# VectorE and ScalarE in the order as written for the first quarter of tokens, key-value products one unit later

## The chip, the cores and the metric

One core of a Trainium2 chip runs the whole program. The time is the device time of one execution in microseconds (us).

## The reference, cut to what matters

Four layers: linear attention, gated MLP, linear attention, gated MLP, each with a layer norm ahead and a residual sum behind, on 2048 tokens of width 1024. Only the first attention layer matters here:

```python
qkv = layernorm(x) @ wqkv                 # 32 heads of 32
phi = lambda t: where(t > 0, t + 1, exp(t)) + 1e-6
kv  = einsum("bhsd,bhse->bhde", phi(k), v)   # summed over all tokens
z   = einsum("bhsd->bhd", phi(k))            # summed over all tokens
o   = (phi(q) @ kv) / (phi(q) @ z + 1e-6)
x   = x + o @ wo
```

## The kernel before

Tokens are handled in tiles of 128; four tiles are a quarter. A "unit" is eight TensorE matmuls that project one tile onto 512 columns. Every unit is followed by a tick, and `later.at(n, f)` runs `f` n ticks on. In the first quarter of layer 0 there are eight value units, then eight key units; after the second key unit of a tile comes its key-value step, eight small matmuls that add phi(k)ᵀ v of that tile.

```python
def phi(self, ps, out):                       # after each key unit
    nc.scalar.activation(out=e, in_=ps, func=ACT.Exp)                    # L243
    nc.vector.tensor_scalar(out=e, in0=e, ..., op0=ALU.min, op1=ALU.add) # L244, first half
    nc.vector.scalar_tensor_tensor(out=out, in0=ps, ..., in1=e, ...)     # L245, second half
...
def k_sum(t):                                 # column sums for z, on GpSimd
    nc.gpsimd.tensor_tensor(out=ksum, in0=ksum, in1=pk[t], op=ALU.add)   # L299 (first one L297)
...
def v_unit(q, j, c):                          # ScalarE copies a value unit out of PSUM
    nc.scalar.activation(out=va[t][...], in_=project(f"v{c}", q, j), func=ACT.Copy)  # L304
...
def last(j):                                  # second key unit of a tile
    u_j = u[QT + j]
    return lambda: (u_j(), later.at(3, lambda: kv_step(q * QT + j)))
...
for i in range(QT, self.ST):                  # layer norms of tiles 4 to 15, three ticks apart
    self.ln_at((4 if l == 0 else 2) + 3 * (i - QT), l, i, 2)
...
run(first)                                    # eight value units
run(k_then_kv(0))                             # eight key units
run(column_major(v_unit, 1))
run(k_then_kv(1))
```

A layer norm is two statistics instructions and an aggregation on VectorE (L136, L141), two small ones on ScalarE for the reciprocal deviation (`rstd`, L143, L144), and a scaling on VectorE (L152). Where nothing says otherwise, a scheduler decides at build time in which order each engine gets its instructions, by its own estimate of when each could run. A region with `manual_schedule(engines=...)` makes those engines take the instructions of the region in the order in which the program issues them; what stands outside the region is still placed by the scheduler. TensorE writes its products to a memory called PSUM; the PSUM tiles for units come from a pool of four. "The head" is the start of the kernel, up to the transposes of the first four token tiles. In the profile lines `x` is the input, `xn` a normalized tile, `tp` and `xnT` its transposes, `ps` a unit's result, `e` the exponential in phi, `pkv` a buffer of phi(k) and v, `kv` the key-value products and `ksum` the column sums.

Of the kernel before, what the change touches and what calls it, by code (L numbers as in the profile page):

```python
# [15 lines left out]
QT = 4  # L16
# [62 lines left out]
class _Net:  # L79
# [184 lines left out]
    def layer_A(self, l, last_ln):  # L264
        nc, G, KT, D = self.nc, self.G, self.KT, self.D
        ring, later = self.ring, self.later
# [40 lines left out]
        def kv_step(t):  # L307

            for g in range(G):
                b, i = divmod(g, NW // P)  # L310
                nc.tensor.matmul(kv[b][:, i * P:(i + 1) * P], lhsT=pk[t][:, g * P:(g + 1) * P],  # L311
                                 rhs=va[t][:, g * P:(g + 1) * P], start=(t == 0 and i == 0),
                                 stop=(t == self.ST - 1 and i == NW // P - 1),
                                 skip_group_check=True)
# [86 lines left out]
        def column_major(f, q):  # L401
            return [lambda j=j, c=c: f(q, j, c) for c in range(H) for j in range(QT)]
# [16 lines left out]
        def k_then_kv(q):  # L419
            u = column_major(k_unit, q)  # L420

            def last(j):
                u_j = u[QT + j]
                return lambda: (u_j(), later.at(3, lambda: kv_step(q * QT + j)))

            return u[:QT] + [last(j) for j in range(QT)]

        def run(*lists):

            n = max(len(u) for u in lists)  # L430
            for i in range(n):
                for u in lists:
                    if i < len(u):
                        u[i]()
                        later.tick()
# [7 lines left out]
        first = column_major(v_unit, 0)  # L443
        if l == 0:

            first = [first[c * QT + j] for c, j in ((0, 0), (0, 1), (1, 0), (0, 2), (1, 1), (1, 2),
                                                    (0, 3), (1, 3))]
        run(first)
        run(k_then_kv(0))
        run(column_major(v_unit, 1))  # L450
        run(k_then_kv(1))
        run(column_major(k_unit, 2))
# [154 lines left out]
```

## Time and profile before

| | before |
|---|---|
| device time, median of 6 runs | 1644.81 us (1644.57 to 1646.01) |
| profiled span | 1642.6 us |
| TensorE busy | 1632.7 us |
| TensorE's wait for phi of the first quarter | 0.6 us |
| TensorE's wait at the transposes of token tile 3 | 1.5 us |

How to read it: TensorE has work in all but 9.9 us of the span, so the table of its waits, not the busy shares of the others, says what there is to win. A line of that table names who waited, the line and releaser, and then total, number and longest of the waits. The prediction shows these lines. The wait in the head: this is the timeline of the kernel before around it (start, duration, engine, line, operation, and in brackets the idle time before and who ended it):

```profile
16.45 0.69 DVE L136 BATCH_NORM_STATS2 stats<-x 128x6 f32<-128x512 bf16 x1 [1.33 <-DMA x<-in_A_x_dram]
17.07 0.19 DVE L141 BATCH_NORM_AGGREGATE mv<-st 128x2 f32<-128x12 f32 x1
...
18.46 0.62 PE L203 MATMUL tp<-ident,xn 128*128 128x128 bf16 x8 [1.53 <-DVE xn L152]
```

VectorE stands still for 1.33 us for the input of tile 4 (written to `stats`), and only then aggregates tile 3 (read from `st`), whose statistics were long there. TensorE then waits for tile 3.

### The profile page before, as it was taken

The page shows a single profiled execution, that of the slowest core. Times are in us where ns is not written, and L with a number is a line of the kernel's source. Part 1 is how long each engine was busy: PE and PEld are TensorE (multiplying, and loading weights), DVE is VectorE, ACT ScalarE, POOL GpSimd, SP SyncE. Part 2 cuts the span into 40 slices and gives each one's busy share as a digit, 9 for nine tenths or more (in the row PEclk, how much of TensorE's full clock was granted, in tenths as well). Part 3 has the DMA queues.
Part 4 walks back from the last instruction along what each step waited for, and adds up shares of the span by engine and source line. Part 5 has one row for each costly group of instructions (what it writes and reads, how often), then busy time and mean ns, then how long its engine had stood idle before and what let it go on. Part 6 is the DMA issues. An engine that isn't in the chain of part 4 may idle for free.

```text
span 1642.6 us, 18754 instructions
## 1 busy us (share of the span) xinstructions
PE 1632.7 (99%) x7786; PEld 749.8 (46%) x7786; DVE 575.8 (35%) x931; ACT 371.7 (23%) x699; POOL 196.3 (12%) x102
## 2 busy tenths in 40 slices
PE   8999999999999999999999999999999999999999
PEld 4444444444444444444444444444444444444444
DVE  8654876222211311322146457841112112211111
ACT  4356602101110110111033675121011101101110
POOL 0355800000000000000013566000000000000000
PEclk9999999999999999999999999999999999999999
DMA  9113726456445544644530146374544564455452
GB/s 283 25 52 78 181 42 171 149 166 195 152 138 167 160 151 157 183 151 142 166 77 1 58 104 154 55 202 145 176 143 153 160 198 150 144 158 163 154 160 71
DMA packets 298052, 227.18 MB, mean 138 GB/s; under 512 B 103152, under 2 KB 296048, under 8 KB 297968
## 3 DMA queue, kind: packets, MB, share of 16 engines
q1 hardware_dynamic: 293216, 221.80, 46.7%
q10 hardware_dynamic: 4752, 4.20, 0.8%
q8 instruction: 61, 1.00, 0.3%
q14 instruction: 23, 0.19, 0.0%
HBM read 197.13 MB, written 4.19 MB: 123 GB/s over the span
## 4 chain that ended last, share of the span: by engine, by line
PE 94%; ACT 2%; DVE 1%; issue 1%; ACTq 0%
PE pg L508 24%; PE pu L508 24%; PE acc L532 23%; PE ps L284 16%; PE ps L390 7%; PE kv L311 1%; ACT e L347 1%; ACT e L346 1%; PE acc_last L532 0%; DVE den L361 0%; DVE pq L349 0%; ACT e L348 0%; PE fold L378 0%; DVE T L384 0%; DVE xn L152 0%
## 5 line engine op out<-in xcount | busy, mean ns | idle before, releaser
L508 PEld LDWEIGHTS <-t 128*128 128x128 bf16 x3584 | 350.7, 98 | 422.8
L508 PE MATMUL pg<-xnT,t 128*128 128x512 bf16 x1792 | 423.3, 379 | 0.0
L508 PE MATMUL pu<-xnT,t 128*128 128x512 bf16 x1792 | 423.3, 379 | 0.0
L532 PE MATMUL acc<-t,hT 128*128 128x512 bf16 x1764 | 382.5, 379 | 0.0
L514 DVE TENSOR_TENSOR hT<-pu,rg 128x512 bf16<-128x512 f32 x224 | 154.7, 691 | 571.6 <-PE pu L508 571.6
L284 PE MATMUL ps<-t,xnT 128*128 128x512 bf16 x1536 | 341.0, 379 | 1.0 <-DVE xnT L206 0.6
L513 ACT ACTIVATE rg<-pg 128x512 f32<-128x512 f32 x224 | 133.6, 596 | 737.5 <-PE pg L508 737.4
L532 PEld LDWEIGHTS <-hT 128*128 128x128 bf16 x1820 | 178.1, 98 | 209.0
L284 PEld LDWEIGHTS <-xnT 128*128 128x128 bf16 x1536 | 148.7, 98 | 175.2 <-issue 1.8
L390 PE MATMUL ps<-T,pqT 128*128 128x512 bf16 x512 | 111.2, 379 | 0.0
L143 ACT ACTIVATE rstd<-mv,eps 128x1 f32<-128x1 f32 x64 | 18.9, 295 | 339.9 <-DVE mv L141 339.9
L297 POOL CAST ksum<-pkv 128x1024 f32<-128x1024 bf16 x2 | 2.3, 1136 | 682.8 <-DVE pkv L245 682.8
L547 DVE TENSOR_TENSOR xo<-x,acc 128x512 bf16<-128x512 f32 x31 | 21.3, 687 | 170.3 <-PE acc L532 170.3
L136 DVE BATCH_NORM_STATS2 stats<-x 128x6 f32<-128x512 f32 (+1 forms) x120 | 78.4, 671 | 2.0 <-DMA x<-in_A_x_dram 1.3
L390 PEld LDWEIGHTS <-pqT 128*128 128x128 bf16 x512 | 50.1, 98 | 60.4
L356 POOL TENSOR_TENSOR prod<-pq,zrow 128x1024 f32<-128x1024 bf16 x32 | 68.1, 2127 | 58.2 <-DVE den L361 35.9
L544 DVE TENSOR_TENSOR x<-x,acc 128x512 f32<-128x512 f32 x32 | 21.6, 676 | 149.5 <-PE acc L532 148.4
L299 POOL TENSOR_TENSOR ksum<-ksum,pkv 128x1024 f32<-128x1024 f32 x30 | 65.5, 2182 | 68.9 <-DVE pkv L245 67.7
L244 DVE TENSOR_SCALAR e<-e 128x512 f32<-128x512 f32 x64 | 52.8, 825 | 48.8 <-ACT e L243 48.5
L349 DVE SCALAR_TENSOR_TENSOR pq<-ps,e 128x512 bf16<-128x512 f32 x64 | 42.9, 670 | 68.3 <-ACT e L348 68.2
L367 POOL TENSOR_TENSOR pq<-pq,den 128x1024 bf16<-128x1024 bf16 x32 | 61.2, 1912 | 10.5 <-issue 4.0
L243 ACT ACTIVATE e<-ps 128x512 f32<-128x512 f32 x64 | 38.1, 596 | 70.8 <-PE ps L284 68.0
(46 smaller groups left out, 490.4 us busy)
## 6 DMA issues: line engine op xcount, KB each, us to landing
t<-in_B_W_gate_dram SPq DMA_DIRECT2D x56, 1024.0 KB, 6.6
t<-in_B_W_up_dram SPq DMA_DIRECT2D x56, 1024.0 KB, 5.3
t<-in_B_W_down_dram SPq DMA_DIRECT2D x64, 896.0 KB, 5.1
t<-in_A_wqkv_dram SPq DMA_DIRECT2D x11, 1024.0 KB, 5.1
t<-in_A_wo_dram SPq DMA_DIRECT2D x4, 1024.0 KB, 5.2
out_dram<-xo ACTq DMA_DIRECT2D x31, 128.0 KB, 2.2
x<-in_A_x_dram SPq DMA_DIRECT2D x15, 256.0 KB, 8.2
t<-in_A_wqkv_dram SPq DMA_DIRECT2D x2, 512.0 KB, 4.9
```

Of the source, the lines that this page charges most:

```text
L136: self.nc.vector.bn_stats(out=stats[:, c, :], in_=src[:, c * fmax:(c + 1) * fmax])
L244: nc.vector.tensor_scalar(out=e, in0=e, scalar1=1.0, scalar2=1e-6, op0=ALU.min, op1=ALU.add)
L284: nc.tensor.matmul(ps, lhsT=self.xnT[l, l_q][:, kt, j * P:(j + 1) * P], rhs=w[:, kt, :], start=(kt == 0), stop=(kt == KT - 1))
L299: nc.gpsimd.tensor_tensor(out=ksum, in0=ksum, in1=pk[t], op=ALU.add)
L349: nc.vector.scalar_tensor_tensor(out=pq[:, c * NW:(c + 1) * NW], in0=ps, scalar=0.0, in1=e, op0=ALU.max, op1=ALU.add)
L356: nc.gpsimd.tensor_tensor(out=prod, in0=pq, in1=zrow, op=ALU.mult)
L367: nc.gpsimd.tensor_tensor(out=heads(pq), in0=heads(pq), in1=den[:, :].unsqueeze(2).to_broadcast([P, D // HD, HD]), op=ALU.mult)
L390: nc.tensor.matmul(ps, lhsT=pqT[sc][:, g, j * P:(j + 1) * P], rhs=T[g // 2][:, g % 2, n2 * NW:(n2 + 1) * NW], start=(g == 0), stop=(g == G ...
L508: nc.tensor.matmul(ps, lhsT=w[:, kt, fi * P:(fi + 1) * P], rhs=self.xnT[l, q][:, kt, :], start=(kt == 0), stop=(kt == KT - 1))
L513: nc.scalar.activation(out=rg, in_=pg, func=ACT.Relu)
L514: nc.vector.tensor_tensor(out=h[:, fi, :], in0=pu, in1=rg, op=ALU.mult)
L532: nc.tensor.matmul(ps[:, 0:n], lhsT=hT[ft // 4][:, ft % 4, j * P:(j + 1) * P], rhs=wd[:, k, i * n:(i + 1) * n], start=(ft == 0), stop=(ft ...
```

## The change

The intent: keep the layer norms of later tiles from standing in front of phi in VectorE's queue, and give phi one unit more before TensorE uses it.

```diff
             def last(j):
                 u_j = u[QT + j]
-                return lambda: (u_j(), later.at(3, lambda: kv_step(q * QT + j)))
+                return lambda: (u_j(), later.at(4, lambda: kv_step(q * QT + j)))
 ...
-        run(first)
-        run(k_then_kv(0))
+        def quarter0():
+            run(first)
+            run(k_then_kv(0))
+
+        if l == 0:
+            with self.tc.manual_schedule(engines={mybir.EngineType.DVE,mybir.EngineType.Activation}):
+                quarter0()
+        else:
+            quarter0()
         run(column_major(v_unit, 1))
```

## The prediction

> **What bounds the kernel now.** I read the page's busy shares first, then the waits of TensorE over the whole span, then busy time by stretch for the first 70 us, then the timeline around the one wait that the change can reach. The page's first lines:
>
> ```profile
> span 1642.6 us, 18754 instructions
> ## 1 busy us (share of the span) xinstructions
> PE 1632.7 (99%) x7786; PEld 749.8 (46%) x7786; DVE 575.8 (35%) x931; ACT 371.7 (23%) x699; POOL 196.3 (12%) x102
> ```
>
> TensorE is busy 1632.7 of 1642.6 us: 9.9 us idle in all, and the matmuls are the same after the change. So no reordering of other engines can gain more than 0.6% of the time. TensorE's waits, whole span:
>
> ```profile
> PE idle L174 <- DVE zero L171: 2.1, 1, 2.1
> PE tp L203 <- DVE xn L152: 1.5, 1, 1.5
> PE fold L378 <- DVE T L384: 1.5, 4, 0.4
> PE kv L311 <- DVE pkv L245: 0.6, 1, 0.6
> ```
>
> (Columns: total, times, longest.) The first two lie in the head (start and transposes of the first four token tiles), the third after the query projections. Only the fourth, one wait of 0.6 us of a key-value product for phi(k), is of the stage that the change touches. Busy time by stretch (window: length, then busy time of each engine):
>
> ```profile
> 18.00:27.00 9.00, 8.54 (x46) 4.19 (x47) 8.96 (x22) 5.10 (x16) 0.00 (x0) 1.00 1.07 371
> 27.00:36.00 9.00, 9.00 (x44) 4.03 (x43) 8.96 (x21) 4.08 (x12) 0.00 (x0) 1.00 1.20 216
> 36.00:48.00 12.00, 11.40 (x77) 6.06 (x76) 11.55 (x22) 4.54 (x13) 8.17 (x4) 1.00 0.64 110
> 48.00:58.00 10.00, 10.00 (x48) 4.56 (x47) 0.55 (x1) 4.13 (x8) 0.00 (x0) 1.00 0.28 53
> ```
>
> From 18 to 48 us VectorE (third busy figure) is full: it runs the layer norms of tiles 5 to 15 far ahead of their use, woven between the phi of the first eight key units; then it is idle for 9.4 us. TensorE loses 0.60 us in 36:48, nothing in 27:36 and 48:58. How the loss arises (timeline):
>
> ```profile
> 39.15 4.89 POOL L299 TENSOR_TENSOR ksum<-ksum,pkv 128x1024 f32<-128x1024 f32 x2 [0.45 <-DVE pkv L245]
> ...
> 41.56 0.50 DVE L244 TENSOR_SCALAR e<-e 128x512 f32<-128x512 f32 x1
> ...
> 41.98 2.35 DVE L152 TENSOR_SCALAR xn<-x,mv,rstd 128x1024 bf16<-128x1024 bf16 x1
> ...
> 44.24 0.68 DVE L245 SCALAR_TENSOR_TENSOR pkv<-ps,e 128x512 bf16<-128x512 f32 x1
> ...
> 44.98 0.40 PE L311 MATMUL kv<-pkv 128*128 128x128 bf16 x4 [0.60 <-DVE pkv L245]
> ```
>
> A layer-norm scaling (L152), not needed for many microseconds, stands between the two halves of the last phi. It takes 2.35 us instead of the 0.55 us it takes elsewhere, because GpSimd's column sum (L299) is running; the phi ends at 44.92 and the product starts 0.60 us late.
>
> **What the Trainium skill says.** "SBUF — State Buffer", section Who interferes with whom: VectorE's 2-port modes, open to tensor_scalar, take a port pair shared with GpSimd as an exclusive lock, and the later one fully blocks; VectorE work with at most one SBUF input outside those modes is not affected. The trace agrees: L152 above ends just after GpSimd's pair of sums (39.15 + 4.89 = 44.04), while the second half of phi (L245, one input in PSUM) stays at 0.68 us beside GpSimd. "PSUM — Partial Sum Buffer", section Engine vs sequencer instructions: ScalarE and VectorE queues are strict FIFO. Agreed, and it carries this case: the L245 that TensorE awaited stood behind L152.
>
> **The change, part by part.** I compared the instruction orders before and after. TensorE: the same products, each tile's eight key-value matmuls one unit of eight matmuls later. GpSimd and SyncE: unchanged orders. VectorE and ScalarE: different only up to the last layer norm of layer 0; the second attention layer shifts only its key-value products, where no wait was seen. Nothing is added or removed, so the sum is a change of TensorE idle time before about 65 us.
>
> Durations I use, from timeline rows: a unit of TensorE 1.725 us (ScalarE exps 57.50, 59.23, 60.95), a kv step 0.44 (37.48 to 37.92), exp 0.60, first half of phi 0.42, second half 0.69 (together about 1.07 in a row), a layer norm on VectorE 1.71 per tile (scalings at 23.48, 25.20, 26.91), GpSimd's sum 2.15.
>
> (a) First key units. VectorE now does only tiles 4 and 5 early, then waits for the exp of key unit 0. Unit n of k ends at 27.3 + 1.725n. Phi 0 ends about 29.1, phi 1 30.9; then tile 6's norm in between (stats 30.8 to 32.1, rstd, scaling 33.4), phi 2 to 4 by 36.7, tile 7's norm to 39.3, then phi 5 40.4, phi 6 41.4. GpSimd starts the sum of tile 1 at 40.7, so the first half of phi 7 (ready at 41.4) is held to 43.2 as above, and phi 7 ends about 43.9.
>
> (b) Products. With the extra unit kv0 to kv3 stand at 39.4, 41.5, 43.7, 45.9, after phi 4 to 7 at 36.7, 40.4, 41.4, 43.9: slack 2.7, 1.1, 2.3, 2.0. No wait: **-0.60 us**. Without the extra unit kv1 would stand near 39.8, before its phi at 40.4: some 0.6 us lost. So the reordering alone would gain nothing; the extra unit is what pays.
>
> (c) The norms pushed back. Tiles 8 to 15, eight times 1.71 to 1.77 us = 14 us, now start at 43.9 instead of running from 20 us on, and end near 59.7 instead of 48.7. Their outputs have time: tile 8 is first used by unit 24 of TensorE, near 70 us. But ScalarE's order interleaves their rstd pairs with the copies of the next eight value units, and a copy frees one of four PSUM tiles for the unit four later. Adding up: copies of value units 1, 2, 3 start near 46.3, 48.4, 52.2 and must end by 49.8, 51.5, 53.2 (slack 3, 2.5, 0.4 us); the copies of units 4 to 6 wait for the stats of tiles 12, 13, 14 and end near 55.0, 56.8, 58.6, against key units that want to start at 54.9, 56.7, 58.4. That is a tie: VectorE's 1.71 us per tile against TensorE's 1.725 per unit. My sum gives **+0.2 us** new idle; one microsecond of later VectorE would make it about +1.1, one earlier 0. Tile 8's scaling also meets GpSimd's last sum (45.4 to 47.5) and is blocked about 0.7 us, which is in the sum.
>
> (d) Phi of the next key units waits for the norms' end: first one near 61.3, needed at 62.1. No loss.
>
> Sum: -0.60 + 0.2 = **-0.4 us**: 1644.9 us.
>
> **The rivals.** (1) ScalarE's copies held behind the pushed-back statistics become TensorE's new wait (step c), +1 to +2 us: for it, the tie; against it, the same weave ran at 24 to 27 us without any wait of TensorE. It would make 1645.5 to 1646.5. (2) GpSimd's lock hits a first half of phi worse than I reckon, so kv3 waits: 2.0 us slack is nearly a whole sum, so less likely; 1645 to 1646. (3) The wait goes away with nothing new: 1644.7. (4) The head's 1.5 us wait (a tile-4 statistics op put ahead of tile 3's aggregation) might be thought cured; the order of those instructions is the same in both, so it stays. (5) The transposes into the next quarter come late: tile 7's is scaled at 39.3, lands 3.3 us later (median of DMA landings of xnT), 42.6, and is needed at 46.3: no.
>
> **Range and chances.** The three runs before spread 1.4 us (1644.61 to 1646.01), as much as the effects. From rival 3 with half the spread below, to rival 1 with some above: 1643.6 to 1646.6. Two per cent is 33 us, more than three times all idle time of TensorE, so faster is impossible by this and slower would need a stall that no step has.
>
> **What would show it.** Right: no wait of kv (L311) for L245 in TensorE's waits; GpSimd's first column sum near 36.9 instead of 37.46; VectorE idle from about 26 to 28 us and full from 44 to 60; the 1.5 us wait of tp unchanged. Wrong: TensorE waits of L284 for ScalarE's pkv copies (L304) between 50 and 60 us larger than 0.5 us in sum, or a kv wait still there. The prediction as a whole fails if TensorE's idle time changes by more than about 1.5 us either way.

## The result, and the profile after

The changed kernel took 1644.03 us (median of 6, 1643.65 to 1644.63), the kernel before 1644.81 us. The ratio, 0.9994 with a 95% interval of 0.9982 to 1.0007, is the mean time of the one kernel's fast runs over that of the other's of the same rounds, so not quite the ratio of these medians. The interval holds 1: the clocked time alone does not prove a gain. A second set of five runs gave 1643.86 us against 1645.07 us (ratio 0.9993, 0.9979 to 1.0007). The traces are sharper than the clock. TensorE's waits in the changed kernel, whole span:

```profile
PE idle L174 <- DVE zero L171: 2.1, 1, 2.1
PE tp L203 <- DVE xn L152: 1.7, 2, 1.3
PE fold L378 <- DVE T L384: 1.5, 4, 0.4
PE ps L284 <- DVE xnT L206: 0.3, 1, 0.3
```

The wait of L311 for L245 is gone and no wait for L304 has come. (Of the two waits of `tp`, 1.30 us is at tile 3 and 0.38 us at tile 1.) Busy time by stretch (window: length, then TensorE, weight loads, VectorE, ScalarE and GpSimd, then granted clock, busy share of the DMA engines and GB/s):

```profile
18.00:27.00 9.00, 8.22 (x44) 4.03 (x46) 3.57 (x9) 4.44 (x11) 0.00 (x0) 1.00 1.07 371
27.00:36.00 9.00, 8.96 (x42) 4.07 (x42) 6.44 (x13) 3.26 (x7) 0.00 (x0) 1.00 0.77 150
36.00:48.00 12.00, 11.93 (x79) 6.44 (x80) 11.19 (x20) 3.75 (x10) 7.52 (x4) 1.00 0.14 26
48.00:58.00 10.00, 9.95 (x47) 4.55 (x47) 9.84 (x23) 4.61 (x16) 0.00 (x0) 1.00 0.70 132
```

VectorE's work has moved: 3.57 us instead of 8.96 in 18:27, and 9.84 instead of 0.55 in 48:58. TensorE's busy figure must not be compared across the two traces: this one has 7632 matmul records where the other has 7786, for the same program, so some are missing. I use start times instead. Timeline of the changed kernel around the products:

```profile
39.47 0.61 PE L311 MATMUL kv<-pkv 128*128 128x128 bf16 x8
...
40.71 6.64 POOL L299 TENSOR_TENSOR ksum<-ksum,pkv 128x1024 f32<-128x1024 f32 x3 [2.73 <-DVE pkv L245]
...
41.53 1.63 DVE L244 TENSOR_SCALAR e<-e 128x512 f32<-128x512 f32 x1
...
43.19 0.69 DVE L245 SCALAR_TENSOR_TENSOR pkv<-ps,e 128x512 bf16<-128x512 f32 x1
...
45.99 0.61 PE L311 MATMUL kv<-pkv 128*128 128x128 bf16 x8
```

GpSimd still delays VectorE here (1.63 us for the first half of the last phi, where the same step took 0.42 us just before it). But that phi ends at 43.88 us, 2.1 us before its product at 45.99.

**The stage as a ruler.** From the start of the tile-3 transposes (`tp`) to the first key-value product of the second quarter TensorE does the same work in both kernels, apart from the one extra unit (8 matmuls at 0.2158 us, 1.73 us) that now comes first. The lines before (the `tp` at 18.46 is shown further up; the line at 44.00 is the first half of the product that waits) and after:

```profile
44.00 0.39 PE L311 MATMUL kv<-pkv 128*128 128x128 bf16 x4
...
67.66 0.61 PE L311 MATMUL kv<-pkv 128*128 128x128 bf16 x8
```

```profile
18.72 0.62 PE L203 MATMUL tp<-ident,xn 128*128 128x128 bf16 x8 [1.30 <-DVE xn L152]
...
68.88 0.61 PE L311 MATMUL kv<-pkv 128*128 128x128 bf16 x8
```

Before: 67.66 - 18.46 = 49.20 us. After: 68.88 - 18.72 = 50.16, less 1.73 = 48.43 us. So the change is worth **0.77 us** in the stage where it acts. The `tp` of tile 3 happened to start 0.26 us later in this trace; the spans differ by 0.5 us, which is 0.77 less 0.26.

### The profile page after: what moved, and what is told of

Same layout as the page of the kernel before. It is cut to its first block, busy times and chain, and to the rows that moved or that the text cites. A ratio compares the mean times of both kernels' runs of the same rounds, so it can differ in the third digit from the quotient of the medians.

```text
span 1642.1 us, 18601 instructions
## 1 busy us (share of the span) xinstructions
PE 1625.1 (99%) x7632; PEld 749.7 (46%) x7786; DVE 577.7 (35%) x931; ACT 371.1 (23%) x699; POOL 195.6 (12%) x102
## 4 chain that ended last, share of the span: by engine, by line
PE 95%; ACT 2%; issue 1%; DVE 1%; DMA 1%; SPq 0%; ACTq 0%
PE pu L515 23%; PE pg L515 23%; PE acc L539 23%; PE ps L284 17%; PE ps L390 7%; PE kv L311 1%; DMA x<-in_A_x_dram 1%; ACT e L347 1%; ACT e L346 1%; PE acc_last L539 0%; DVE den L361 0%; ACT e L348 0%; DVE pq L349 0%; PE fold L378 0%; SPq L251 0%
## 5 line engine op out<-in xcount | busy, mean ns | idle before, releaser
L284 PE MATMUL ps<-t,xnT 128*128 128x512 bf16 x1500 | 338.1, 379 | 2.4 <-DVE xnT L206 0.3
L284 PEld LDWEIGHTS <-xnT 128*128 128x128 bf16 x1536 | 148.6, 98 | 174.9 <-issue 1.6
```

Of the source, the lines that this page charges most:

```text
L284: nc.tensor.matmul(ps, lhsT=self.xnT[l, l_q][:, kt, j * P:(j + 1) * P], rhs=w[:, kt, :], start=(kt == 0), stop=(kt == KT - 1))
```

## The experiments

All gave correct results. "Stage" is the ruler above, less 1.73 us where the products have the extra unit. The mean differences are those of the fast runs against the kernel before, run in the same rounds.

| run | runs | median us | mean difference us | stage us |
|---|---|---|---|---|
| before | 9 and 9 | 1644.78 and 1645.07 | 0 | 49.20 |
| the change, again | 5 | 1643.86 | -1.00 | 48.42 |
| order as written alone | 5 | 1644.42 | -0.11 | 48.91 |
| extra unit alone | 5 | 1644.23 | -0.65 | 48.43 |
| before, GpSimd sums later | 4 | 1645.06 | +0.20 | 48.43 |
| change + 1 GpSimd op | 1 | 1644.45 | | 48.89 |
| change + 3 GpSimd ops | 1 | 1645.85 | | 50.45 |
| change + one chain from the head | 5 | 1642.54 | -2.21 | see text |
| extra unit + chain in the head | 5 | 1642.63 | -2.34 | see text |

Only the last two rows have a ratio to the kernel before whose 95% interval excludes 1: 0.9987 (0.9974 to 0.9999) and 0.9986 (0.9973 to 0.9998). For all other rows the stage in the trace carries the reading, not the clock.

### Which of the two parts pays

`order_only`: the changed kernel with the old distance of the products.

```diff
-                return lambda: (u_j(), later.at(4, lambda: kv_step(q * QT + j)))
+                return lambda: (u_j(), later.at(3, lambda: kv_step(q * QT + j)))
```

> The change without the extra unit: VectorE and ScalarE in the order as written for the first quarter, key-value products where they were before. My theory (the extra unit is what pays, the order alone does not): kv1 now stands near 39.9 us, ahead of the end of its phi at about 40.6, so TensorE waits 0.6 to 0.9 us at kv1, and the time is that of the kernel before within 0.4 us. Rival (the order as written is what takes the wait away): no wait of L311, and about 0.8 us less than before.

Timeline of that run at the second product:

```profile
39.79 0.39 PE L311 MATMUL kv<-pkv 128*128 128x128 bf16 x4
...
40.48 0.40 PE L311 MATMUL kv<-pkv 128*128 128x128 bf16 x4 [0.30 <-DVE pkv L245]
```

There is a wait, at the product my theory named, but it is shorter than the 0.6 to 0.9 us that I had expected: 0.30 us listed, 0.48 us lost in the stage (why the two differ is said further down). The reason is in the two lines: the step goes out as four matmuls, a wait, and four more. The first four use the columns of the tile's first key unit, whose phi was long done; only the last four need the phi that I compared with the step's start. The stage is 48.91 us, so the order alone is worth 0.29 us and leaves 0.48 us (48.91 - 48.43) on the table.

`late_only`: the kernel before with `later.at(4, ...)` and nothing else.

> The kernel before with only the extra unit ahead of the key-value products; VectorE and ScalarE order left to the scheduler. My theory: kv3 moves to about 45.7 us, the phi that it needs still ends near 44.9, the wait of 0.6 us is gone, and the gain of the change (span 0.5 to 0.8 us shorter) is there without the order as written. Rival (both parts are needed): a wait of L311 for L245 of at least 0.3 us is left.

Timeline of that run at the last phi and the last product:

```profile
42.55 0.67 DVE L245 SCALAR_TENSOR_TENSOR pkv<-ps,e 128x512 bf16<-128x512 f32 x1
...
43.14 1.08 DVE L152 TENSOR_SCALAR xn<-x,mv,rstd 128x1024 bf16<-128x1024 bf16 x1
...
45.63 0.61 PE L311 MATMUL kv<-pkv 128*128 128x128 bf16 x8
```

The wait is gone and the stage is 48.43 us (68.52 - 18.36 - 1.73), the same as with both parts. **The extra unit alone gives the whole gain of the stage.** One reserve: the scheduler answered by also moving the scaling that stood inside the last phi to behind it (43.14 us above), and the phi ended at 43.22 us where I had expected 44.9, so this run does not have exactly VectorE's old order. With that order the last phi ended at 44.92 us and the product now stands at 45.63 us, which would have been enough; that is argued, not run.

### Is GpSimd's hold the cause of the wait before?

`sums_later`: the kernel before, VectorE's order untouched, products where they were; GpSimd's first four sums wait for the phi of tile 4.

```diff
         def k_sum(t):
+            if l == 0 and t < QT:
+                return
-            if t == 0:
+            if t == 0 or (l == 0 and t == QT):
                 nc.gpsimd.tensor_copy(out=ksum, in_=pk[t])
+                for i in range(t):
+                    nc.gpsimd.tensor_tensor(out=ksum, in0=ksum, in1=pk[i], op=ALU.add)
```

> The kernel before, with GpSimd's first four column sums held until the fifth tile's phi is there (sum of tile 4 first, then 0 to 3; result the same up to rounding). Same VectorE order as before. If GpSimd's hold on the shared port is the cause of the wait: the layer-norm scaling that took 2.35 us takes 0.55 us, the wait of 0.6 us at kv3 is gone with neither part of the change, span about 0.8 us shorter, unless the later sums hold up phi near 70 us. If VectorE's fullness alone is the cause: the wait stays near 0.6 us.

```profile
42.53 0.55 DVE L152 TENSOR_SCALAR xn<-x,mv,rstd 128x1024 bf16<-128x1024 bf16 x1
...
42.98 0.69 DVE L245 SCALAR_TENSOR_TENSOR pkv<-ps,e 128x512 bf16<-128x512 f32 x1
```

The same scaling in the same place now takes 0.55 us instead of 2.35, no product waits, and the stage is 48.43 us with neither part of the change. So the wait before was GpSimd's hold. The extra unit puts the product behind that hold; the order as written takes the scaling out of the phi, whose first half is then held itself, but for a shorter time (the phi ends at 43.88 us in the changed kernel, 44.92 before). The run is no faster, though (its profiled span is 0.8 us longer than before); its waits of TensorE show what was paid back.

```profile
PE tp L203 <- DVE xn L152: 1.7, 1, 1.7
...
PE ps L284 <- DVE pkv L245: 0.4, 1, 0.4
```

The pushed-back sums now hold up phi beyond 66 us until a unit lacks a PSUM tile (at 94.34 us), and tile 3 came 0.64 us later than in the trace before. The edit does not touch that: VectorE stood still 1.48 us for the input of tile 4, and tile 3 behind it, as in the head of the kernel before.

### How near was the new wait?

The prediction's rival 1 was that ScalarE's copies, held behind the pushed-back statistics, would become TensorE's new wait. To find the slack I made VectorE late without touching an order: one or three more multiplications on GpSimd, which hold scalings as above.

```diff
                 nc.gpsimd.tensor_tensor(out=ksum, in0=ksum, in1=pk[t], op=ALU.add)
+            if l == 0 and t == QT - 1:
+                for _ in range(1):        # 3 in the second run
+                    nc.gpsimd.tensor_tensor(out=zrow, in0=pk[t], in1=pk[t], op=ALU.mult)
```

> The changed kernel with one more multiplication on GpSimd right after the fourth column sum (into a tile that is not yet in use, result unharmed); orders of TensorE, VectorE and ScalarE the same. It measures how near step (c) is to its edge. In the trace of the changed kernel the copies of value units 4 to 6 end about 0.35 us before TensorE needs their PSUM tiles. Theory: GpSimd works from about 47.4 to 49.4 us, the scaling of tile 9 (48.34 in the changed kernel) is held and VectorE is late by 0.7 to 1.0 us from there on; TensorE then loses 0.35 to 0.65 us between 53 and 60 us, in waits of L284 for L304. Rival (the pushed-back norms have slack of more than 1 us): TensorE loses nothing.

> As the one before with three multiplications. Theory: VectorE late by 1.7 to 2.3 us in all, TensorE loses that less 0.35 us: 1.3 to 2.0 us before 60 us. Rival (slack of more than 1 us): 0 to 1 us.

Timeline of the run with one, then the waits of TensorE in the run with three:

```profile
46.73 2.08 POOL L302 TENSOR_TENSOR zrow<-pkv 128x1024 bf16<-128x1024 bf16 x1
...
47.78 1.32 DVE L152 TENSOR_SCALAR xn<-x,mv,rstd 128x1024 bf16<-128x1024 bf16 x1
```

```profile
PE ps L284 <- ACT pkv L307: 1.7, 2, 1.4
```

With one, the scaling is 0.77 us longer and the stage grows by 0.46 us (48.89 - 48.43). With three, the stage grows by 2.02 us, just above the 1.3 to 2.0 us that I expected: two scalings are longer, by 0.77 and 1.55 us (1.32 and 2.10 in place of 0.55), and 2.32 less the slack found below is 2.01. Both losses are waits of a unit for a value copy, the line that was L304. So the slack was 0.77 - 0.46 = 0.31 us: rival 1 is a real mechanism that the change missed by a third of a microsecond. (Both runs were taken once, state unknown; the stage is read inside one trace.)

### A version that beats both

The wait in the head comes from a region that ends too early: the head's own region orders tiles 0 to 3 among themselves, but tile 4's first statistics belong to no region (before) or to another one (after), and the scheduler puts them ahead of tile 3's aggregation. `one_chain` is the changed kernel with one region for VectorE around the head and the first quarter.

```diff
+        dve = ExitStack()
         if l == 0:
+            dve.enter_context(self.tc.manual_schedule(engines={mybir.EngineType.DVE}))
             self.head()
 ...
             with self.tc.manual_schedule(engines={mybir.EngineType.DVE,mybir.EngineType.Activation}):
                 quarter0()
+            dve.close()
```

> The changed kernel with one more thing: VectorE in the order as written from the head on, so that the statistics of tile 4 no longer stand ahead of the aggregation of tile 3. Expected: tile 3's aggregation starts near 15.6 instead of 17.33 us, TensorE's wait of 1.3 us at the transposes of tile 3 (tp L203) is gone or below 0.2 us, time about 1.3 us below the changed kernel: near 1642.7. Rival: tile 3's input or the weights arrive too late, and the wait only changes its name (to a DMA): gain below 0.5 us.

```profile
15.36 0.21 DVE L141 BATCH_NORM_AGGREGATE mv<-st 128x2 f32<-128x12 f32 x1
...
16.77 0.62 PE L203 MATMUL tp<-ident,xn 128*128 128x128 bf16 x8
...
17.54 1.28 DVE L136 BATCH_NORM_STATS2 stats<-x 128x6 f32<-128x512 bf16 x2
```

The aggregation starts at 15.36 us, the transposes at 16.77 with no idle time before them. It took 1642.54 us, 1.3 to 1.5 us below the changed kernel's two medians. The table gives no stage for it, as two matmuls that preceded the transposes now follow them: it reads 67.36 - 16.77 - 1.73 = 48.86, and 48.43 without those two (0.43 us). Its table of TensorE's waits has one line that no other run has, `PE ps L284 <- ACT rstd L144: 1.3, 1, 1.3`. It lies at 8.93 us, in front of the second half of the very first unit. The six other traces that list a wait there put it down to the landing of a weight and have these matmuls start between 8.20 and 9.12 us, so it is more likely that than the ScalarE instruction named; that is argued, not shown. It does not set the time of tile 3: the transposes of tile 1 follow at 9.79 us, and in the other runs at 9.45 to 10.07.

`one_chain_late` is the kernel before with the extra unit and that region kept open only to the end of the first eight value units, so that key units stay with the scheduler.

> The kernel before with the extra unit ahead of the key-value products and VectorE in the order as written from the head to the end of the first eight value units only; key units left to the scheduler. If the order as written of the key units adds nothing beside the extra unit: no wait of L311, no wait of tp L203 for tile 3, time that of the run with one chain (1642.5) within 0.4 us. Rival (that order is needed once the head is earlier): a wait of L311 or L284 of at least 0.3 us comes back.

1642.63 us, with no wait of L311; its TensorE waits in the head are

```profile
PE ps L284 <- DVE xnT L206: 0.6, 2, 0.3
PE ps L284 <- DMA t<-in_A_wqkv_dram: 0.6, 1, 0.6
PE tp L203 <- DVE xn L152: 0.2, 1, 0.2
```

The last one, of 0.2 us, belongs to tile 1 (at 9.46 us), not to tile 3. The two versions cannot be told apart by time. With the extra unit in place, the order as written of the key units buys nothing measurable.

### The change once more

`after_again` is the changed kernel unedited, for its spread.

> The changed kernel again, for its spread on the chip of the others. Expected 1643.6 to 1644.7 us, 0.5 to 0.9 us below before; TensorE's wait at tile 3's transposes between 0.9 and 1.8 us, as it varies with the landing of tile 4's input; from there to the first key-value product of the second quarter 50.16 us within 0.1.

Most of it came about: 1643.60 to 1644.53 us, but 1.0 us (mean) to 1.2 us (median) below before in place of 0.5 to 0.9; the wait at tile 3 was 1.73 us in this trace (1.30 in the first one), and the stretch from there 69.31 - 19.16 = 50.15 us.

## Why the prediction was right, point by point

What came about is the prediction's rival 3: the wait went away and nothing new came. Both terms of the sum were mis-sized in the same direction, so the 1644.9 us foretold was too high (1644.03 and 1643.86 measured). That the measured time lies inside the range says little: the range of 3 us also holds "no change". It was even wider at its lower end than its own recipe gives: rival 3 with half the spread below is 1644.7 - 0.7 = 1644.0, not 1643.6. What carries the prediction is that its steps can be found in the trace.

- **The bound and the cap.** Right. TensorE's idle time was all there was to win.
- **Step (a), the new times of phi.** Right to 0.3 us: GpSimd's first sum at 36.95 us (36.9 foretold), VectorE idle before 28.21 us, the last phi at 43.88 (43.9), its first half held by GpSimd from 41.53 to 43.16 (41.4 to 43.2).
- **Step (b), the products.** They stand at 39.47, 41.64, 43.82 and 45.99 us (39.4, 41.5, 43.7, 45.9), without a wait. The term was mis-sized: the wait is worth 0.77 us, not 0.60. The listed idle time starts only at the modelled end of the last matmul, and that lies 0.16 us beyond the spacing of the stream (records of 0.379 us every 0.216 us). The step is cut in two, the first half at 44.00 us, the second at 44.98; four small matmuls take 0.22 us, so without the wait the second half would have come at 44.22.
- **"The reordering alone would gain nothing"** failed in size. It gained 0.29 us in the stage: it took away a wait worth 0.77 us, not 0.60, and brought one worth 0.48 us, not 0.6, because only half of a product step depends on the phi that I compared it with. That the extra unit is what pays was right, and stronger than I put it: it pays all of the stage's gain by itself.
- **Step (c), the +0.2 us.** Mis-sized: it measured 0. The copies of value units 4 to 6 end at 54.72, 56.44 and 58.15 us where I had 55.0, 56.8 and 58.6; the units that need their PSUM tiles would start at 55.07, 56.80 and 58.53 (46.44 us plus five, six, seven units). The mechanism is as described, as the added GpSimd work showed. Tile 8's scaling was blocked 0.70 us by GpSimd's last sum (1.25 in place of 0.55), as reckoned.
- **Step (d).** Right: the first phi of the next quarter ends at 60.86 us (61.3 foretold).
- **The sum.** The terms measured -0.77 and 0 where I had -0.60 and +0.2, so -0.77 in place of -0.4 us. The clocked means moved by -0.91 and -1.00 us in the two sets of rounds. The 0.1 to 0.2 us beyond the stage lie within the spread of single runs (1 us), and I leave them open; the start of tile 3 alone varied from 18.16 to 19.16 us over the runs that keep the old head.
- **Two slips in the working.** Of the lines shown, the L245 at 44.24 us is no proof that a second half of phi is unaffected beside GpSimd, since the sums had ended at 44.04; the one at 40.30 us, also 0.68 us long, is, as it lies inside them. And rival 1 would make 1645.7 to 1646.7 us by its own terms (1644.9 less 0.2 plus 1 to 2), not 1645.5 to 1646.5.

## What to carry to other kernels

When one engine is busy 99% of the time, read the few waits it has left, and for each ask which single instruction stood in front of the releaser; giving the consumer one more step of distance can be as good as reordering the producer, and here did not use up the slack of the value copies (in `late_only` each copy from 49.73 us on still waits 1.13 us for its unit). Work that is moved later does not vanish: find the next consumer that shares a queue with it and reckon its slack, here a third of a microsecond. A region that fixes an order protects only what lies inside it, so look at what the scheduler puts at its edges.

## What the Trainium skill lacked or had wrong

- "SBUF — State Buffer", section Who interferes with whom: nothing wrong. The scaling of 0.55 us took 2.35, 1.32 and 2.10 us beside GpSimd and 0.55 again once GpSimd was moved; the statistics instruction, which that section does not name, stayed at 0.63 to 0.69 us beside GpSimd's sums.
- "PSUM — Partial Sum Buffer", section Engine vs sequencer instructions: the strict queue agrees with the traces here (before, the L245 came at 44.24 us, behind the L152 held from 41.98). The section does not say what such a queue costs through a third engine: statistics 0.77 us late on VectorE made a ScalarE copy late and so TensorE by 0.46 us.
- No page says by how much an idle time listed between matmuls falls short of what TensorE loses (it would belong to "Perfetto Trace Analysis"): in these traces by 0.16 to 0.18 us a wait (0.60 listed, 0.77 lost; 0.30 and 0.46 to 0.48; two waits of 1.70 together and 2.02).
